# A new order of every engine's queue in a fused attention and feed-forward kernel, with other scratch tiles for one weight conversion

## The chip, the cores and the metric

One core of one Trainium2 chip runs the kernel. The metric is the device time of one execution in microseconds (us). Smaller is better. The kernel before took 1261.1 us (median of three runs, 1261.0 to 1261.12).

## The reference

Four batches of 12608 queries, keys and values of width 128 meet 49 agents. The attention result goes, row by row, through a feed-forward block with a SoLU activation.

```python
a2k = sm(agents, k)          # softmax(scale * agents @ k.T), per batch
agent_v = a2k @ v
q2a = sm(q, agents)
x = q2a @ agent_v            # 50432 rows of 128
h = x @ w_in                 # 1024 wide
sm = softmax(h)
solu = h * sm
ln = (solu - mean(solu)) / sqrt(var(solu) + 1e-06) * g_ln
out = ln @ w_out             # 50432 rows of 128, float32
```

`w_in` and `w_out` are float64 and come to the chip as pairs of 32-bit words. The kernel turns them into float32 with integer operations of its own.

## The kernel before, in words

The rows are cut into 394 tiles of 128. A tile's main path goes through five engines: PE multiplies it into two halves of a 1024-wide PSUM tile `ph` (`c_h`, L956), DVE takes the row maximum and writes a scaled copy to `e` (`c_max`, L984), ACT takes the exponential back into `ph` (`c_exp`, L991), DVE multiplies the two into one of six tiles `u_a` to `u_f` (`c_u`, L999), and ACT sums squares (`c_sq`, L1020). For eleven of thirteen tiles POOL then splits `u` into two float16 halves `f` (`c_f0`, L1007, and `c_f1`, L1010), SP has them transposed by DMA into `x` (`c_x`, L1014), and PE multiplies by the output weights (`c_w`, L1048). The other two of thirteen are transposed on PE (L1027) and copied into `t` (L1032). DVE scales four tiles at a time into an output buffer (`c_fin`, L1093), of which there are two, each for eight tiles, and SP stores it (`c_out`, L1099).

Before the first tile can run, the head of the kernel computes `agent_v` of batch 0 (`phase_a`, L567). It goes through twelve chunks of 1024 keys and one shorter one. For chunk c: SP loads k (`kload`, L585) and v (`vload`, L591; three small loads at L596 for the last chunk); PE multiplies k by the agents (`p1_mm`, L602); DVE takes a running maximum (L607, L614); ACT the exponential (`p1_exp`, L628); PE transposes it (`p2_t`, L635); ACT copies that out (`p2_et`, L645); PE multiplies it by v (`p2_mm`, L655); DVE adds it to `av` (`p2_ev`, L664). In the head k lies in the eight `x` tiles and v in the eight `t` tiles, so v of chunk 8 may be loaded once `p2_mm` of chunk 0 is done, v of chunk 9 after `p2_mm` of chunk 1, and so on up to chunk 12. Results of PE lie in four PSUM banks `px`; each product or transpose takes one and holds it until it is read. When all thirteen chunks are added up, `f1` (PE, L711), `f2` (ACT, L714), `f3` (PE, L745), `f4h` (ACT, L751) and `f4l` (DVE, L755) form the matrix that `c_h` uses.

The head also holds the conversion of both weights (L399, DVE, ACT and POOL), the centring of the output weights (POOL, L453, L462 and L472, with the PE product `mean`, L466, and DVE's `peak`, L477), and the softmax of the first eight tiles of queries (`phase_b`, L850: PE L864, DVE L870 and L876, ACT L880, POOL L894 and L898, PE L905, copy into `pT` L911).

The conversion `pair_f64` (L378) needs four scratch tiles, called s, a, e and m. For `w_in` they are `e_a`, `e_b`, `u_a`, `u_b`. For `w_out` they are `e_a`, `e_b`, `u_e`, `u_f`: it shares two with `w_in`, so all of its steps wait for the conversion of `w_in` (`cin` in L1132). The first two `c_max` write `e_a` and `e_b`, and the first six `c_u` write `u_a` to `u_f`, so L1174 and L1177 name both conversions, `cin + cout`, as what they wait for.

The order in which each engine gets its work is written out: `STEPS` (L25) is a packed list with one entry for each of 7003 steps, and `Plan.run` (L198) issues them in that order. Some steps may go to one of two engines, and a bit of the entry says which. Where the plan expects PE to idle in the head, `idle` (L1106) puts small products of constants into PE's queue, called fills here (L1109); their number follows from the plan. The kernel before has 57 of them.

Of the kernel before, what the change touches and what calls it, by code (L numbers as in the profile page):

```python
# [30 lines left out]
    "b0(`=m&fKE6V~f@8p08Nx2DgncV(swk+r(>(OCShXEV2suMe9o<k{`T@bI2?>|WN2RaFNg0Qh5D{U+RRO~&s|bv^&#JL~fA{noB-w?}-sNX#p%"
    "bk~>Krnq8qczs+FZf(zWWn$)tg6JV)k!t_o;v}fin1f>7t!}?-cxG`Yg^xCYRM%v`JG0bxHzZFP$A(Uf^8mjypESfKW#oA-MmiSOhBnSUiPiV("
    "!Be1<x7DiW{ijQ5^SR7);9vTUKj>~eX^_h2-)#(?D~UmT3-te^pSX;8vc1~95iL%hYbqxl(e{x;EQ9YK#k!QkUDK@tGO#)8kS7y^`;{HUpzm&a"
    "-|osNEOwvNxVo89kqIy{{cFFD-;>RkO^rw6HeE+OxM|S2kL2T^uevQ`8DBiPNH))XB&HS`O{)#S*)EgM`hm=5kRMJ0%PMv(op-cadsNGw8UL+&"
    ";Y3BW17KdOGP#I8ebnXd#SFTMrHsp-A;#}BEhI6Si{5QIZwObP-ku&Exgj(=rt7xf`TF|s=oxXUBxGxK26^Uz7(dZ~shhqep_;VqSh3*J1o-*?"
    "G4!G8oYdLf@>QQcdT3f1=olh;gS`X2aj@-mrcQ@?S{LtBZ6_1P(aW^uT73&D<m;WAJ`?d|B$VgMG0(9jBd<QuUlSbw;PRc0?S3#7HuYwd^X~?T"
    "ul;xg293CTW9F*yu&ZiM|NPsv?V-$s6pY|=58;d%^zBX8&D_-bYzy6*ba-^u>1?uCy=iFkaJ54UJRg^5FIJXjo!6@_Fq<Rlr{|{U%*MEwOnc|_"
    "GFLd9w%Y>n`0yQ}+A~f&<%ZCN*SJz2(N_3xS1p!?$GY}-*yx|WlASk%awFFY>{{_aHU!469|`^Bh|v}}scBv(T4IK@nq0kI-+g#gN&=4E@Y0#-"
    "nmG8N9KKepH=O;IA738_#{_5w<57!jL<XvzRbvgup^hD*s?iwMs2af714gbcpJI#2h*jDMLXPuG7+p0V35{k+9viXyfFpHuf`fVWQc8Vyo;mA{"
    ")wWbzM@MJ8(lyd}ELW_!vLRKg{H|s|KbrGTx1Gk~PQva#Z39xG);kK8vYscOqhiIjwh_-n$@<*~nKQH4Yye^7{KV2+@B;cKaM^BpknQQ0N1XRF"  # L40
    "%k!sR|GdMlvkxlGih;-Qk-X8|u+mm_5K<-N_}Z1m8<Ly0Mmu^f;<^UMXy8P1E&t&kbQ~)c?&g#nuatTFALceDBAE{#+BVzj@2A?r);5K;b~aOU"
    "i=SgnRU>-QPu^B9O;z51kWKi!mdX>&Q~;zl^c`1{di<<)uRfbmCHyUOw&_*(kqWHd1Po5O0tWQqS?}3do9);C)AXGtv~m+#bN}csHD?n2AI^8C"
    "30tz3Xj<J^x{8hB0N2z_LfDu$Tz;InO4PLj+fis|%|*PouPu*n>Z{c@*UjPZvK5R^YSY*9%GGzy*#*$ycPidbE>1eyNB;eP9>2mtqVHPa$OIkE"
    "-LuJT`%Odi(FBeXPH@}-dhHM=rJaH8h`KIvxzRm7qio*EWCw`8mI>SBK*x5)R?wQ6mUaZDC%TWfT8HKDClry{b>f}Wn7Hjc5KqZNiWq2;=+vaP"
    "bN1|{Zr&1Bdhn5n(F40C*P!lSoLp2#&8Au9T=<CS#(nnt+&M9T&$ODnnJysDsl3X$#iUYs(Q!m%Gu>TBonCwZZ#~<>@A{XOU;W683QsxWgzUU#"
    "a94LgBt7qIYl*>Sza<-4#Ld+!k&UUA-6g+uHgMChIB8k!-&X}Rj(ISAD{+M^z#|_CIC^7Czw^Bl`DpX|a3~!)?zn0X*ns0Ye3sQ8yZ-*)HM?aS"
    "2c|k@)kFP>D++qYjQV8=C182{FlzQh4*QQ!>N~uoZb94j-LEC=F7@b<;%F9Fb8Qd^W_yR5j(hf{!)Kd%>Df2{1HeAlo1L|WdiFO59a?gKt1DjV"
# [188 lines left out]
def kernel(  # L236
# [864 lines left out]
    def F(f, *x):  # L1101
        return lambda *y: f(*x, *y)
# [195 lines left out]
```

## Time and profile before

| what | us |
|---|---|
| median of three runs | 1261.1 |
| the profiled execution's own time | 1258.08 |
| span of that execution, first to last instruction | 1256.3 |
| first `c_max` starts, in the span | 57.83 |

The profiled execution was 3.0 us shorter than the median. Its span is counted from its first instruction. An engine's row of a view gives a start, a duration, the engine, the line, the operation, the tile written and the tiles read. In views by window, each engine's busy time in the window stands with the number of its instructions. SPq is the queue of DMA issues.

### The profile page before, as it was taken

Reading aid. Unit: us, or ns where it says so; the run is one execution under the profiler, and the core shown is the slowest. Engines: PE = TensorE matmul, PEld = TensorE weight load, DVE = VectorE, ACT = ScalarE, POOL = GpSimd, SP = SyncE. Lnnn points to the kernel's source line nnn. Section 1 sums busy time; section 2 is a strip of 40 time slices with the busy share of each in tenths; the row PEclk is TensorE's granted clock in tenths of the full one; section 3 lists DMA queues with packets and bytes.
Section 4 is the critical chain, followed back from the end, with each engine's and each line's share of the span. In section 5 each row is a group of like instructions: output and inputs, shape, how many; then the busy total and the mean of one; then the engine's idle time right before and its main releaser. Section 6 shows DMA issues by size and latency. Waiting matters only on the chain.

```text
span 1256.3 us, 36417 instructions
## 1 busy us (share of the span) xinstructions
PE 1211.7 (96%) x14324; PEld 935.4 (74%) x14324; DVE 1202.1 (96%) x2296; ACT 1181.9 (94%) x2210; POOL 1120.3 (89%) x891
## 2 busy tenths in 40 slices
PE   8889999999999999999999999999999999999998
PEld 4667777777777877777778777777777777777778
DVE  5799999999999999999999999999999999999997
ACT  5499899999999999999999999899999999999998
POOL 3488898999999998889999989889898999999995
PEclk9999999999999999999999999999999999999999
DMA  9589999999999999999999999999999799899897
GB/s 366 202 195 242 229 246 232 239 249 201 202 210 239 243 231 250 246 257 221 229 205 207 247 243 227 240 259 217 230 231 195 173 200 198 189 218 199 176 209 169
DMA packets 721516, 281.41 MB, mean 224 GB/s; under 512 B 692672, under 2 KB 696256, under 8 KB 721344
## 3 DMA queue, kind: packets, MB, share of 16 engines
q1 hardware_dynamic: 721344, 279.08, 103.5%
q8 instruction: 112, 1.84, 0.6%
q14 instruction: 60, 0.49, 0.1%
HBM read 79.67 MB, written 25.82 MB: 84 GB/s over the span
## 4 chain that ended last, share of the span: by engine, by line
PE 27%; DVE 21%; ACT 19%; issue 14%; POOL 10%; DMA 9%; SPq 0%; POOLq 0%; DVEq 0%; ACTq 0%
PE px L1048 11%; ACT ph L991 8%; PE ph L956 7%; DVE e_b L984 4%; DVE e_a L984 4%; ACT sq_b L1020 4%; ACT sq_a L1020 3%; PE px L655 2%; PE px L602 2%; DVE u_c L999 2%; POOL f_a L1010 2%; DVE u_d L999 1%; DVE u_b L999 1%; DVE u_a L999 1%; DVE u_e L999 1%
## 5 line engine op out<-in xcount | busy, mean ns | idle before, releaser
L984 DVE TENSOR_SCALAR_CACHE_REDUCE e_a<-ph,nk 128x1024 f32<-128x1024 f32 x197 | 251.8, 1278 | 7.4 <-PE ph L956 6.4
L984 DVE TENSOR_SCALAR_CACHE_REDUCE e_b<-ph,nk 128x1024 f32<-128x1024 f32 x197 | 251.7, 1278 | 3.9 <-PE ph L956 3.3
L991 ACT ACTIVATE ph<-e_a,nm 128x1024 f32<-128x1024 f32 x197 | 219.2, 1113 | 15.2 <-DVE e_a L984 13.8
L991 ACT ACTIVATE ph<-e_b,nm 128x1024 f32<-128x1024 f32 x197 | 219.3, 1113 | 8.2 <-DVE e_b L984 7.3
L999 DVE SCALAR_TENSOR_TENSOR u_d<-e_b,cb,ph 128x1024 f32<-128x1024 f32 x66 | 84.2, 1276 | 2.1 <-ACT ph L991 1.7
L999 DVE SCALAR_TENSOR_TENSOR u_a<-e_a,cb,ph 128x1024 f32<-128x1024 f32 x66 | 84.1, 1274 | 1.8 <-ACT ph L991 1.4
L999 DVE SCALAR_TENSOR_TENSOR u_c<-e_a,cb,ph 128x1024 f32<-128x1024 f32 x65 | 82.8, 1274 | 2.2 <-ACT ph L991 1.9
L999 DVE SCALAR_TENSOR_TENSOR u_e<-e_a,cb,ph 128x1024 f32<-128x1024 f32 x65 | 82.9, 1275 | 1.3 <-ACT ph L991 1.1
L999 DVE SCALAR_TENSOR_TENSOR u_b<-e_b,cb,ph 128x1024 f32<-128x1024 f32 x65 | 83.0, 1276 | 1.0 <-issue 0.3
L999 DVE SCALAR_TENSOR_TENSOR u_f<-e_b,cb,ph 128x1024 f32<-128x1024 f32 x65 | 82.8, 1274 | 0.9 <-ACT ph L991 0.4
L1048 PE MATMUL px<-wh,x_c 128*128 128x128 f16 x672 | 70.9, 219 | 2.9 <-DMA x_c<-f_e 2.2
L1048 PE MATMUL px<-wh,x_a 128*128 128x128 f16 x672 | 70.3, 219 | 3.0 <-DMA x_a<-f_c 1.2
L1048 PEld LDWEIGHTS <-x_c 128*128 128x128 f16 x1008 | 61.9, 98 | 13.5 <-DMA x_c<-f_e 3.0
L1048 PEld LDWEIGHTS <-x_a 128*128 128x128 f16 x1008 | 61.5, 98 | 14.0 <-DMA x_a<-f_c 1.8
L1048 PE MATMUL px<-wh,x_b 128*128 128x128 f16 x672 | 71.3, 219 | 0.0
L1048 PEld LDWEIGHTS <-x_b 128*128 128x128 f16 x1008 | 61.4, 98 | 12.9 <-issue 4.9
L1048 PE MATMUL px<-wh,x_h 128*128 128x128 f16 x656 | 69.3, 219 | 1.7 <-DMA x_h<-f_a 1.7
L1048 PEld LDWEIGHTS <-x_d 128*128 128x128 f16 x984 | 60.5, 98 | 13.8 <-issue 2.7
L1048 PEld LDWEIGHTS <-x_e 128*128 128x128 f16 x984 | 60.2, 98 | 14.1 <-issue 3.8
L1048 PEld LDWEIGHTS <-x_h 128*128 128x128 f16 x984 | 60.5, 98 | 13.6 <-DMA x_h<-f_a 2.2
L1048 PE MATMUL px<-wh,x_d 128*128 128x128 f16 x656 | 68.9, 219 | 1.1 <-ACT ek_b L628 0.4
L1048 PE MATMUL px<-wh,x_e 128*128 128x128 f16 x656 | 68.9, 219 | 0.8 <-DMA x_e<-f_a 0.6
(455 smaller groups left out, 4731.9 us busy)
## 6 DMA issues: line engine op xcount, KB each, us to landing
qt_a<-in_qT_dram SPq DMA_DIRECT2D x24, 512.0 KB, 5.0
qt_b<-in_qT_dram SPq DMA_DIRECT2D x24, 512.0 KB, 5.1
out_dram<-ob_a SPq DMA_DIRECT2D x24, 512.0 KB, 4.0
out_dram<-ob_b SPq DMA_DIRECT2D x24, 512.0 KB, 3.6
kt_b<-in_kT_dram SPq DMA_DIRECT2D x18, 512.0 KB, 4.8
kt_a<-in_kT_dram SPq DMA_DIRECT2D x18, 512.0 KB, 5.4
vt_b<-in_v_dram SPq DMA_DIRECT2D x18, 512.0 KB, 5.2
vt_a<-in_v_dram SPq DMA_DIRECT2D x18, 512.0 KB, 4.6
```

The costliest lines, as they stand in the source:

```text
L602: nc.tensor.matmul(px[h * AP2 : (h + 1) * AP2, :w], ag_sb[:, b, :], kt[:, o : o + w], start=True, stop=True)
L655: nc.tensor.matmul(px[h * AP2 : (h + 1) * AP2, :C], eT[:w, o + h * AP2 : o + (h + 1) * AP2], vt[:w, t, :], start=all(z[0] != h for z in mm ...
L956: nc.tensor.matmul(ph[:, sl], w, m[:, sl], start=(q == 0), stop=(q == len(mm) - 1))
L984: nc.vector.tensor_scalar(out=nhs[x], in0=phs[x], scalar1=nks[k][:, j : j + 1], scalar2=None, op0=ALU.mult, op1=ALU.min, accum_out=nms[x])
L991: nc.scalar.activation(out=phs[x], in_=nhs[x], func=AF.Exp, scale=-1.0, bias=nms[x], accum_out=rs_[R]["S"][:, j : j + 1])
L999: nc.vector.scalar_tensor_tensor(out=u, in0=nhs[x], scalar=scal(x)[:, 4:5], in1=phs[x], op0=ALU.mult, op1=ALU.mult, accum_out=su)
L1010: nc.gpsimd.tensor_tensor(out=fs[x][:, 1, :], in0=us[x][0], in1=fs[x][:, 0, :], op=ALU.subtract)
L1020: nc.scalar.activation(out=sq, in_=u, func=AF.Square, bias=su, scale=-float(DF), accum_out=rs_[R]["Q"][:, j : j + 1])
L1048: nc.tensor.matmul(po, ut, wt[:, kf, :], start=(q == 0), stop=(q == len(mm) - 1))
```

## The change

The scratch of `w_out`'s conversion becomes `u_c`, `u_d`, `u_e`, `u_f`. It no longer shares a tile with that of `w_in`, so its steps drop `cin` as a dependency, `c_max` of the first two tiles waits for `cin` alone, and so does `c_u` of tiles 0 and 1; `c_u` of tiles 2 to 5 waits for `cout`. The packed list is another one over the same 7003 steps.

```diff
 STEPS = (
...
 )
...
-            for k, tg in zip("saem", er + (ur[:2] if names == "in" else ur[4:])):
+            for k, tg in zip("saem", er + ur[:2] if names == "in" else ur[2:]):
...
-    cout = [chain(c_out_f[h], OUTC, [res["wout"]] + cin) for h in range(2)]
+    cout = [chain(c_out_f[h], OUTC, [res["wout"]]) for h in range(2)]
...
-        MX[x] = op("D", F(c_max, x, ku - 1, t % UB), 1.2, ..., [H[x, 0], H[x, 1], NK] + (cin + cout if x < 2 else []))
+        MX[x] = op("D", F(c_max, x, ku - 1, t % UB), 1.2, ..., [H[x, 0], H[x, 1], NK] + (cin if x < 2 else []))
...
-        U[x] = op("D", F(c_u, x), 1.205, ..., [EX[x], CB[b]] + used + (cin + cout if x < UBUF else []), after=[U.get(x - 1)])
+        U[x] = op("D", F(c_u, x), 1.205, ..., [EX[x], CB[b]] + used + (cin if x < 2 else cout if x < UBUF else []), after=[U.get(x - 1)])
```

Unpacked, the two lists put the loads of the head on SP in this order (k and v with the chunk; q0 the first queries, wi and wo the weights):

```
before: wi k0 k1 k2 q0 k3 k4 k6 v6 k5 wo k7 v0 k8 v1 k9 v2 k10 v3 v4 v5 k11 k12 v7 v8 v9 v10 v11 v12 q1 q2
after:  wi k0 k1 q0 k2 k4 k3 k6 v6 k5 wo v0 k7 v1 v2 k8 v3 k9 k10 v4 k11 v5 k12 v7 v8 v9 v12 v11 v10 q1 q2
```

PE's order in the head (P = p1_mm, T = p2_t, M = p2_mm with the chunk; b0 = L864; pk = the two transposes of L905; a number in brackets is a count of fills):

```
before: [14] P0 P1 [6] b0 T0 P2 [3] T1 P3 [14] T2 P4 T3 P5 [3] T4 P6 T5 P7 M0 pk [4] T6 pk P8 M1 T7 [1] P9 M2 T8 [3] P10 M3 M4 T9 [2] T10
        M5 P11 P12 M6 M7 g1 M8 g3 T11 T12 M9 mean f0 M10 M11 M12 [4] f1 [3] q2
after:  [14] P0 P1 b0 [2] T0 P2 T1 [2] P3 [3] T2 P4 [1] T3 P5 [5] T4 P6 [2] M0 [1] T5 P7 M1 T6 M2 P8 T7 M3 P9 T8 P10 M4 T9 P11 T10 P12
        M5 M6 M7 M8 g1 M9 g3 T12 T11 mean M10 f0 M11 M12 pk pk f1 [3] q2
```

The list after has 33 fills. It puts `pk` and its two copies, both on ACT now, straight ahead of `f1` and `f2`; the second part of the second group's softmax (DVE, L876) behind the first two `c_max`. Behind the head the two lists differ by swaps of near neighbours. Of the steps that may go to either of two engines, DVE gets 16 copies into `pT` (before 20) and 9 into `t` (before 6).

The stores of eight tiles, counted by how many tiles past its last one the latest transpose ahead of a store is: six stores before are 18 or more tiles late (those of tiles 40, 200, 216, 232, 296 and 312), nine after (8, 104, 136, 152, 232, 264, 296, 312 and 328). The store of tiles 200 to 207 goes from 21 to 8.

## Rows read from the trace of the kernel before

**Rows 1.** The page: busy time, share of the span and instructions of each engine.
```profile
span 1256.3 us, 36417 instructions
PE 1211.7 (96%) x14324; PEld 935.4 (74%) x14324; DVE 1202.1 (96%) x2296; ACT 1181.9 (94%) x2210; POOL 1120.3 (89%) x891
```

**Rows 2.** Windows: busy time by engine in each, granted clock, DMA share, GB/s.
```profile
0.00:57.80 57.80, 50.94 (x453) 30.78 (x453) 37.09 (x109) 27.77 (x68) 23.03 (x34) 1.00 0.77 292
57.80:1230.00 1172.20, 1137.77 (x13600) 883.45 (x13599) 1146.98 (x2157) 1133.88 (x2104) 1085.75 (x840) 1.00 1.06 222
1230.00:1256.30 26.30, 23.02 (x275) 21.13 (x272) 18.00 (x33) 20.22 (x39) 11.57 (x18) 1.00 0.70 163
```

**Rows 3.** Windows within the head, the same columns: PE, PEld, DVE, ACT, POOL.
```profile
8.60:27.55 18.95, 18.93 (x131) 9.09 (x132) 13.50 (x36) 11.34 (x28) 6.34 (x6) 1.00 1.04 411
27.55:51.38 23.83, 22.85 (x258) 16.65 (x258) 16.20 (x47) 11.97 (x36) 13.27 (x14) 1.00 0.74 289
36.00:38.00 2.00, 2.00 (x32) 1.49 (x30) 2.00 (x5) 0.66 (x2) 1.06 (x1) 1.00 1.02 418
40.00:42.00 2.00, 2.00 (x26) 1.43 (x27) 0.36 (x2) 1.25 (x3) 1.94 (x3) 1.00 1.07 329
46.00:48.00 2.00, 2.00 (x27) 1.65 (x25) 0.50 (x4) 1.41 (x5) 0.00 (x0) 1.00 0.03 8
```

**Rows 4.** The chain that ended last, in order of time, in the head.
```profile
25.67 1.01 PE px L602 x4
26.68 0.87 PE px L655 x16
...
27.88 0.44 PE ph L1109 x4
...
48.02 2.83 PE px L655 x38
...
51.39 0.46 PE px L711 x2
51.88 0.28 ACT av_dup L714
...
57.26 0.57 DVE logits L876
57.83 1.20 DVE e_a L984 x2
```

**Rows 5.** SP's queue: what its issues waited for, from 27.55 to 45 us.
```profile
SPq L591 <- PE px L655: 5.2, 2, 3.3
```

**Rows 6.** Timeline of the head (chunk 2's exponent, copies, centring), and one copy near the end.
```profile
18.58 0.70 ACT L628 ACTIVATE ek_a<-px,nmp 128x512 f32<-128x512 f32 x1
...
19.77 0.60 PE L635 MATMUL px<-ident,ek_a 128*128 128x128 f32 x4
...
29.24 0.43 DVE L911 COPY pT_b<-px 128x512 f16<-128x512 f16 x1 [0.96 <-PE px L905]
...
39.17 0.57 ACT L911 COPY pT_a<-px 128x512 f16<-128x512 f16 x1
...
50.58 1.25 POOL L472 TENSOR_TENSOR f_e<-f_e,mean_sb 128x512 f32<-128x512 f32 x1
...
1243.33 0.68 DVE L1032 COPY t_e<-px 128x512 f32<-128x512 f32 x1
```

**Rows 7.** Windows behind the head, all engines: the most and the least idle hundred of DVE.
```profile
700.00:800.00 100.00, 95.97 (x1153) 73.75 (x1152) 94.22 (x177) 93.13 (x173) 88.70 (x67) 1.00 1.16 237
1000.00:1100.00 100.00, 95.71 (x1173) 75.66 (x1172) 99.23 (x179) 99.15 (x179) 97.58 (x74) 1.00 0.94 199
```

**Rows 8.** Timeline of SP and DVE around two late stores.
```profile
774.39 0.53 SPq L1099 DMA_DIRECT2D out_dram<-ob_a  x1
774.98 0.42 SPq L1099 DMA_DIRECT2D out_dram<-ob_b  x1
...
779.51 0.69 DVE L1093 TENSOR_TENSOR ob_b<-px,yc 128x512 f32<-128x512 f32 x1 [1.23 <-DMA out_dram<-ob_b]
...
789.95 1.28 DVE L984 TENSOR_SCALAR_CACHE_REDUCE e_a<-ph,nk 128x1024 f32<-128x1024 f32 x1 [1.94 <-PE ph L956]
```

**Rows 9.** Waits of DVE from 58 us to the end: total us, times, longest.
```profile
DVE ob_b L1093 <- DMA out_dram<-ob_b: 1.2, 1, 1.2
```

**Rows 10.** Windows around the first tiles: PE idles, then runs at a lower granted clock.
```profile
57.80:61.70 3.90, 1.64 (x37) 1.42 (x36) 3.90 (x11) 3.26 (x5) 1.45 (x2) 0.98 0.53 165
61.70:65.00 3.30, 3.30 (x14) 1.68 (x14) 2.71 (x5) 3.30 (x8) 3.17 (x2) 0.50 0.21 86
```

More of the change, by code (lines that the diff above doesn't have):

```diff
@@ L31 @@
[L31 to L35, printed above, removed]
@@ L146 @@
[L146 to L150 removed]
+    "c-ozL4@@gtdf)ii_;Pu-x5$||^H@SDL6le)a#@zJ1R=^=j>|fPScFnUsN*`su@FKCAwpQ!YdM4<L=o!{*K#e#B9tPRP~<qS*Fh8^L|Kax<Perp"
@@ new lines @@
+    "L<#kd9E%Xb<#LUg={YlFd&a)6-Sk}^%*>fN=R4oO-|zcQ<8d>dR4S95<rjvY15g#~INxp|+BOMg?a@Yia4RIck6xL}BmMVtja}~p=GyW89raG{"
+    ")xgkTxy;q?RCO%R1k~}Kqp{!$eB#)SCR+yWsoICY<lW_7z*$#*)pT@UcX?ux#qOImM=NzVy%+Bi>hkEr(ad{a@8LslR8v0H<k)|YPgVB;&*atL"
+    "e*M1Q>Wh_c?TowLk5;Ug_uNp;hW9mPmkH@aNast;$U-T@oxFT#_#ySKH#NR`ho4=xjjrv#SH)+++L>~<6C_fOdW)N~+igI<CC&6yIVBRUD&dm="
+    "jgm^q&otyk+YV5Z$xIU&*Cds`q4-IYnoJ!U&z0nV`C1||O-3X)wO8t@dUr2ADgIIunn;}t4*F9QK-tu}pgc<sM&q;5!7<b6?&hKakMF3*r<OZM"
+    "bw@w^QKvE)Cl>sb3wT_uy?L%(RZJQDTIFK!<l-j2Mv#L;2K7+i{c2rv#SeaK^>BS+(VKZc0Olij2Gf?w5|w}Wa(_If@-)Y$=GBwa=TDJkAd}C&"
@@ new lines @@
+    "E4z;@NbTxm+&~bg<xAs@LrckyxWdxhDkJ)b6B?o)0Aqt<cG#~`T!dB0&E4ciVy>fgckArN5Z_r(9uV=v?KZheo1C9Nqf%iY3sA@L(Aq!%>ziBv"
+    "_;Ab^B>Vx7ZmWt=s!mUuPZEuar1k_0r!>UuH-6+<35IvyKav)3Ox^gp>dPM-(Y=n%`s;&aVp6}~zV|fSu5AzWX(!f)db<qKfiq=C<r--}o0;A9"
+    "Z#ys7T)i{5hE7wNJ}RH_;rEn+`k()>eK|SQIyY@q5xoFdToYEG=43>-<eLThg^+RRdHwzL45@eN6n>%#%#dDueEH&TW$U;(H9i_0oB{VsmBaH>"
+    "HuAIw2f$EQ-q>mg*=+}o@a5<)ek+yST3o*It@J*~>aOAq{WEd`gvrKf5Aj?F8obA<mg^=Es`qxcT<Gq*oXOh9fAmf3RX2HNXdUeCUrNOycvF4L"
+    "=%&o)pS~Sh*C}R=9n*t<_T7W2vDK}Wk^QCqKDjP|o0Iim{Mcyl%z(PR3VV;dqSnx41I~%`0Z#dzoENQToq}53GOLIh0Gu{rtJRI4+Nb7?+grn%"
@@ L151 @@
+    "kQQXx;)Z0dJyw7?bWsmONHGMozCe{l{NyvOuFud!A(0SvoC+y%5p^nLa9A;eEozow0*;J*hCpC+At?~b%%_n>^_rkU6jp?M_DTz~bYT(rxq=ug"
+    "AZc`A7mxmmBJZn@*7#z7jvEMj2}N?zg&nnmHg93ev#9;c<JH1uGfmS13=rgVVWGe$WuG}(`%E7hD{2Y}5Q`S@5c)F-yU68ey13==ncfD56($Zr"
+    "2`=op7qnzBA&<j~8XG_M(Hi}gM{9+y^!cMTUa5qAw!upm76$^@F4#F%SUd?kP(`h)LVqcW%fb$75#9Mr&$ghm_hTHb@jT`$j@ATrD=-ePlSCIa"
+    "QNQYFO?W2s)eY0aqqU;Oqp+J(#1{YFM{D%o=V-0a<pdc1|97<Ze*l6(As_"
 )
@@ L1173 @@
             NK = op("D", F(c_nk, ku - 1, x, m), 0.15 * (1 + both(x)), dues[3] + 0.4, [rsum["op", ku - 1], CB[b]])
-        MX[x] = op("D", F(c_max, x, ku - 1, t % UB), 1.2, at(x, DMX + (0.0 if xbar(x) else DMXF), DMXR, DMXL), [H[x, 0], H[x, 1], NK] + (cin + cout if x < 2 else []))
+        MX[x] = op("D", F(c_max, x, ku - 1, t % UB), 1.2, at(x, DMX + (0.0 if xbar(x) else DMXF), DMXR, DMXL), [H[x, 0], H[x, 1], NK] + (cin if x < 2 else []))
         EX[x] = op("A", F(c_exp, x), 1.132, at(x, DEX + (0.0 if xbar(x) else DEXF), DEXR, DEXL), [MX[x], U.get(x - 2), FIN.get(RS0[rgrp[x][0] - 3] // GT - 1 if rgrp[x][0] > 3 else -1)], after=[EX.get(x - 1)])
         used = [T.get((x - UBUF, 0)), T.get((x - UBUF, 1)), SQ.get(x - UBUF), F1.get(x - UBUF)]
-        U[x] = op("D", F(c_u, x), 1.205, at(x, DU_ + (0.0 if xbar(x) else DUF), DUR, DUL), [EX[x], CB[b]] + used + (cin + cout if x < UBUF else []), after=[U.get(x - 1)])
+        U[x] = op("D", F(c_u, x), 1.205, at(x, DU_ + (0.0 if xbar(x) else DUF), DUR, DUL), [EX[x], CB[b]] + used + (cin if x < 2 else cout if x < UBUF else []), after=[U.get(x - 1)])
         SQ[x] = op("A", F(c_sq, x), 1.14, at(x, DSQ + (0.0 if xbar(x) else DSQF), DSQR, DSQL), [U[x]] + ([om] if not x else []))
```

230 lines of the change are left out of this document (110 added, 120 removed).

## The prediction

> **What bounds the kernel now.** I read the page first. Over the whole span PE, DVE, ACT and POOL are busy 96, 96, 94 and 89 per cent [rows 1], so no single engine is to be relieved, and the question is where the idle time lies. The windows answer that [rows 2]. Of DVE's 54.2 us of idle time, 20.7 lie in the head (57.80 less 37.09) and 8.3 in the last 26.3 us. The 1172.2 us between hold 25.2, or 2 per cent. The head is therefore where an order can bring most: up to the first `c_max` none of the 394 tiles has advanced, and each microsecond by which it starts sooner moves the rest by as much, if the rest keeps its pace.
>
> What bounds the head is seen in its windows [rows 3]. In the middle (36 to 38 us) the loads run without a gap, at 418 GB/s, and PE is full too. From 40 us the loads ebb, and at 46 us there are none (8 GB/s); yet PE is full until `f1` at 51.38. So PE ends the head, not the loads, by some 5 us. The chain of waits says the same: products of v (L655) follow on each other up to `f1` [rows 4]. PE was late with them because v comes late in SP's list: v of chunk 0 behind k of chunk 7. The same lateness comes back to SP: two loads of v waited 5.2 us together until an earlier product had freed their tile [rows 5].
>
> **The change, part by part.** I make the sum in the profiled execution's own time, 1258.08 us; the median of the runs is 3.0 us longer, and the same difference is taken off it.
>
> *Loads.* The bytes are the same. Each v moves up by one place, and in the new list v of chunk 12 (three issues), 11 and 10 come in this order. Chunk 12's needs `M4` done, and 11, 10 and the two q loads stand behind it on SP. By then (about 36 us) loads issued earlier still keep DMA full [rows 3], so that the wait need not show. I cost it at nothing, covered by PE's work on chunks 5 to 9; without that cover it is at most the 5.2 us of [rows 5].
>
> *PE up to the product of v's chunk 0.* PE is busy 18.93 of 18.95 us here [rows 3], fills among it: 26 before, 16 after (without the 14 ahead of P0). A fill takes 0.44/4 = 0.11 us [rows 4], so ten fewer are 1.1 us. But they stand where PE waits for an exponent: from an exponent's start on ACT to the transposes that need it go 1.19 us (18.58 to 19.77), and exponents come one by one [rows 6]. With fills gone, mostly the wait remains. Following the new order by these durations, P0 to P7, T0 to T5 and M0 are done at 27.3 instead of 27.55. I take 0.25, with 0 and 1.1 as ends.
>
> *PE from there to `f1`.* Before, this is 23.83 us: 22.85 busy, 0.98 idle [rows 3], and 14 fills, 1.5 us. That leaves 21.3 us of work, which both orders hold (each of P, T and M as often, `pk` too). After, there are no fills. Idle remains where T6 to T9 wait for their exponents: between P of a chunk and its T stand one or two other pieces, a P or M of 1.01 us each [rows 4], against maximum, exponent and 1.19. I allow three waits of 0.25, 0.75 in all: 22.1 us, a gain of 1.75. The ends: nothing if all fills turn into waits, 2.5 if none does and the 0.98 goes too.
>
> *`pk` and its copies.* They move from the middle to just ahead of `f1` and `f2`. PE's part is counted above. On ACT two copies of 0.57 [rows 6] now stand in front of `f2`, which before started 0.5 us behind `f1` [rows 4]. The first starts when the first transposes are out, so about 0.3 us stick out and delay `f2`. Ends: 0 and 1.1, both copies. Waiting behind `f2` are `f3`, `q1` and all of the first tiles.
>
> *DVE ahead of the first `c_max`.* 0.57 us (L876) [rows 4] go behind it, and small steps of 0.4 or so come ahead. As DVE is full from there on, this only changes places: +0.1 for the start, nothing for the end. Centring on POOL, which ends 0.45 us after `f1` starts before (50.58 + 1.25) [rows 4, 6], moves up with the conversion and stays covered by `f1` to `q1`.
>
> *The scratch tiles.* Removed: `w_out`'s wait for `w_in`. It costs and gives nothing by itself; it lets DVE do these steps sooner, under loads. Added: `c_u` of tiles 2 to 5 wait for a conversion done some 20 us earlier, so nothing.
>
> *Steps that changed engines.* DVE loses four copies of 0.43 and gains three of 0.68 [rows 6]: +0.3 us over 1200. ACT and POOL change as little. Nothing.
>
> *All behind the head.* The same work in an order of swapped neighbours. I can't price this from a row, so I bound it: DVE's most idle hundred holds 5.8 us of idle time, its least 0.8 [rows 7]. If one hundred went from one end half way to the other, that is 2.5 us either way. I take 0, as neither direction has a reason.
>
> Sum: 0.25 + 1.75 - 0.3 + 0.1 = **1.8 us** sooner. The profiled execution would take 1256.3 us, the median 1261.1 - 1.8 = **1259.3 us**. Ends from the head alone: 1.1 + 2.5 + 0.1 = 3.7 sooner, and no gain. A measurement of this kernel can tell about 0.2 per cent, 2.5 us, from no change, so my forecast counts as the same.
>
> **The rivals.**
>
> *The head packs tightly.* All fills and waits go, and 3.7 us come off: 1257.4. For it: PE has 24 fewer fills, 2.6 us by themselves. Against it: fills stand in waits, and T still waits for ACT. Chance 0.17.
>
> *A stall far behind goes too.* Two stores of eight tiles were issued side by side at 774 us; DVE waited 1.23 us for an output buffer, and 1.94 us for PE some 10 us later [rows 8]. In the new list the first of them comes 13 tiles sooner. 1.8 + 1.23 + 1.94 = 5.0, so 1256.1. Against it: other stores come late instead. Chance 0.15.
>
> *A new wait eats the head's gain.* `f2` waits the full 1.1 for both copies, and the fills all turn into waits for exponents: 1261.1. Chance 0.14.
>
> *Late stores: slower.* Nine stores come 18 or more tiles late, six before. `c_fin` of a buffer's next use stands in DVE's queue in order, and all main steps of DVE behind it wait with it. Before, one late pair showed the stall, 1.23 + 1.94 = 3.2 us [rows 8]. If two such stalls come on top, 6.3 are lost and 1.8 won: 1265.6. From one on top the result is slower than my forecast, from two it is slower than before by over 0.2 per cent. Against it: DVE waited for a store only once [rows 9], so five of the six late ones cost it nothing. Chance 0.07.
>
> *PE's clock falls in the head.* Behind the first products of tiles PE was idle for 2.26 of 3.9 us, and the next 3.3 us went at a granted clock of 0.50, that is at 1.2 GHz instead of 2.4 [rows 10]. If the missing fills let that happen once in the head, 3.3 us at half speed cost 1.65, and 1260.9 is left. Against it: by my working no wait in the new head is longer than 0.9 us, and before, 0.98 us of idle time in 23.83 left the clock at 1.00 [rows 3]. The Trainium skill (TensorE: Matmul & The Clock Gate, "What's actually happening") speaks against the change here: it calls the throttled clock the default, which activity releases, and fewer fills are less activity; by that rule alone the result would be this rival's. The trace bears the rule out behind the head [rows 10], not in it [rows 3]. Chance 0.05.
>
> *The change doesn't do what it says*: not possible here for the order, as the list is what is issued; for the scratch it would show in nothing.
>
> **How the numbers follow.** The forecast has the remaining 0.42: 0.08 of it faster by over 0.2 per cent (head nearer to its upper end), 0.32 the same, 0.02 slower. Faster: 0.08 + 0.17 + 0.15 = 0.40. Same: 0.32 + 0.14 (gain eaten) + 0.05 (clock) = 0.51. Slower: 0.02 + 0.07 = 0.09. The range takes the forecast with 2.5 us either way, and reaches down to the stall that goes (1256.1) and 1.3 below, as both gains of the head may come together with it: 1254.8. Up it goes to the eaten gain with part of the bound on the rest, 1262.8. Left out are late stores and the far ends, less than 2 in 10.
>
> **What would show it right or wrong.** `f1` should start near 49.4 us instead of 51.39, with P12 done before M5; no wait of SP for a product of v longer than before; the two copies right ahead of `f2`; first `c_max` near 55.9. If DVE's idle time from there to 1230 us stays near 25, the forecast holds. A granted clock below 1.00 ahead of `f1`, `f1` later than 50.5, or waits of `c_fin` for `out_dram` in several places would make it wrong; so would a first `c_max` at 56 with a total that is 3 or more us off.

## The result: the head gained what was forecast, the rest lost several times as much

| | before | after |
|---|---|---|
| median, us (7 runs each) | 1261.1 (1256.85 to 1265.82) | 1268.85 (1265.08 to 1273.63) |
| ratio, 95% interval | | 1.0065 [1.0048, 1.0082] |
| the profiled execution's own time | 1258.08 | 1265.08 |
| its span | 1256.3 | 1263.3 |
| first `c_max` starts | 57.83 | 56.10 |

The time is 7.75 us over that of before, and so outside the forecast's range. The kernel is slower, by 0.65 per cent, and the interval leaves no doubt about the direction. The seven runs of before lie up to 9.0 us apart, so that one pair of times would not have told this.

The page of after, which answers to [rows 1]:

```profile
span 1263.3 us, 36367 instructions
PE 1214.8 (96%) x14300; PEld 937.5 (74%) x14300; DVE 1202.3 (95%) x2295; ACT 1180.4 (93%) x2209; POOL 1121.5 (89%) x893
```

DVE is busy as long as before (1202.3 and 1202.1 us): no work was added. The windows of after, cut at its own first `c_max`, say where it idles. Columns as in [rows 2].

```profile
0.00:56.05 56.05, 48.28 (x428) 29.13 (x429) 37.73 (x109) 28.10 (x70) 23.60 (x34) 1.00 0.79 300
56.05:1230.00 1173.95, 1136.57 (x13523) 882.01 (x13521) 1139.10 (x2142) 1126.79 (x2093) 1079.46 (x836) 1.00 1.04 221
1230.00:1263.30 33.30, 29.96 (x352) 26.33 (x350) 25.49 (x45) 25.48 (x47) 18.49 (x24) 0.99 0.80 172
```

Subtract DVE's busy time from each window. In the head it idles 18.3 us (before 20.7), in the last window 7.8 (8.3). In the middle it idles 34.9 (25.2): all of the loss, 9.7 us, lies there, where the forecast had put nothing. What DVE waited for in the middle (in total, times, longest):

```profile
DVE e_a L984 <- PE ph L956: 10.1, 19, 1.4
DVE pk L718 <- ACT av_dup L714: 4.4, 3, 1.5
DVE av L664 <- PE px L655: 3.7, 2, 3.1
...
DVE ob_a L1093 <- DMA out_dram<-ob_a: 0.7, 1, 0.7
```

The first three lines in the kernel before:

```profile
DVE e_a L984 <- PE ph L956: 6.4, 13, 1.9
DVE pk L718 <- ACT av_dup L714: 1.6, 3, 0.9
DVE av L664 <- PE px L655: 1.2, 1, 1.2
```

The waits for PE and ACT grew, in many places. The wait for a store did not: 0.7 us once, where before it was 1.2 once [rows 9].

The 3.1 us are the longest single wait. SP's queue ahead of it:

```profile
265.78 2.88 SPq L1014 DMA_TRANSPOSE x_d<-f_b  x1
268.77 1.59 SPq L596 DMA_DIRECT2D vt_b<-in_v_dram  x3
270.41 0.58 SPq L843 DMA_DIRECT2D qt_a<-in_qT_dram  x1
271.09 0.38 SPq L1099 DMA_DIRECT2D out_dram<-ob_b  x1
271.56 0.38 SPq L1099 DMA_DIRECT2D out_dram<-ob_a  x1
271.99 1.17 SPq L591 DMA_DIRECT2D vt_a<-in_v_dram  x1
273.25 5.53 SPq L1014 DMA_TRANSPOSE x_e<-f_c  x1
```

The chain that ended last and the timeline show what came of it:

```profile
273.25 9.06 DMA x_e<-f_c
```

```profile
282.35 0.23 PE L1048 MATMUL px<-wh,x_e 128*128 128x128 f16 x1 [3.25 <-DMA x_e<-f_c]
285.15 0.35 DVE L664 SCALAR_TENSOR_TENSOR av<-av,fc_l,px 128x128 f32<-128x128 f32 x1 [3.10 <-PE px L655]
```

Seven plain issues, loads and stores, stand between two transposes. The second transpose lands 9.06 us after its issue began; PE, in order, waits 3.25 us for it, and DVE 3.10 behind PE. In the old list the same plain issues stand in two groups, of five and two, with transposes between.

The granted clock had a part in the 3.10 us:

```profile
283.10:286.50 3.40, 3.40 (x27) 2.50 (x26) 1.13 (x5) 1.36 (x4) 3.32 (x3) 0.50 1.25 278
283.12 1.97 PE L655 MATMUL px<-vt_a,eT_a 128*64 128x128 f32 x16
```

Right behind its wait PE ran at 0.50, that is at 1.2 GHz instead of 2.4. The sixteen products that DVE waited for took 1.97 us; sixteen of the same shape take 1.09 in the head, at 1.00 (35.65 below). So about 0.9 of the 3.10 us came from the clock.

**The head.** The timeline around `f1` in after:

```profile
32.74 1.45 POOL L399 TENSOR_TENSOR u_f<-u_f,u_d 128x512 f32<-128x512 f32 x1
33.24 1.50 DVE L399 SCALAR_TENSOR_TENSOR u_c<-f_d,u_c 128x512 int32<-128x512 int32 x1
...
35.65 1.09 PE L655 MATMUL px<-t_e,kt_b 128*64 128x128 f32 x16 [1.20 <-DVE av L664]
...
49.40 0.58 ACT L911 COPY pT_a<-px 128x512 f16<-128x512 f16 x1 [2.93 <-PE px L905]
49.56 0.46 PE L711 MATMUL px<-ff,av 128*128 128x128 f32 x2
49.88 0.59 ACT L911 COPY pT_b<-px 128x512 f16<-128x512 f16 x1
50.35 0.28 ACT L714 COPY av_dup<-px 128x128 f32<-128x128 f32 x1
...
56.10 1.28 DVE L984 TENSOR_SCALAR_CACHE_REDUCE e_a<-ph,nk 128x1024 f32<-128x1024 f32 x1
```

`f1` starts at 49.56 (before 51.39), and the first `c_max` 1.73 us sooner (1.65 by its start in DVE's timeline, 57.74 before, which the table below uses). That is the forecast's 1.8. SP's waits for products of v went from 5.2 us [rows 5] to 3.9, though the longest is 3.5 where it was 3.3:

```profile
SPq L596 <- PE px L655: 3.9, 2, 3.5
```

From there on the starts of `c_max` (L984) can be set beside those of before, tile by tile; a positive number is time lost. The row is one profiled execution of each kernel.

```
tile        0     36     48     60     84     96    180    204    252    288    393
after    -1.6   -2.4    0.9    0.9    8.2    7.8    9.3    9.2    6.8    7.4    8.8
```

The lead is lost between tiles 36 and 48, and between 60 and 84 some 7 us more.

### The profile page after: what moved, and what is told of

The parts are those of the page before. It is cut to its first block, busy times and chain, and to the rows that moved or that the text cites. A ratio compares the mean times of both kernels' runs of the same rounds, so it can differ in the third digit from the quotient of the medians.

```text
span 1263.3 us, 36367 instructions
## 1 busy us (share of the span) xinstructions
PE 1214.8 (96%) x14300; PEld 937.5 (74%) x14300; DVE 1202.3 (95%) x2295; ACT 1180.4 (93%) x2209; POOL 1121.5 (89%) x893
## 4 chain that ended last, share of the span: by engine, by line
PE 28%; ACT 22%; DVE 16%; POOL 13%; issue 11%; DMA 9%; SPq 0%; POOLq 0%; ACTq 0%; DVEq 0%
PE px L1048 12%; ACT ph L991 9%; PE ph L956 7%; ACT sq_b L1020 4%; ACT sq_a L1020 4%; DVE e_b L984 3%; DVE e_a L984 3%; PE px L655 2%; POOL f_d L1010 2%; PE px L602 2%; POOL f_e L1010 2%; POOL f_c L1010 2%; PE px L1027 2%; DMA x_e<-f_c 2%; DVE u_a L999 1%
## 5 line engine op out<-in xcount | busy, mean ns | idle before, releaser
L984 DVE TENSOR_SCALAR_CACHE_REDUCE e_a<-ph,nk 128x1024 f32<-128x1024 f32 x197 | 251.8, 1278 | 11.1 <-PE ph L956 10.5
L984 DVE TENSOR_SCALAR_CACHE_REDUCE e_b<-ph,nk 128x1024 f32<-128x1024 f32 x197 | 251.8, 1278 | 3.9 <-PE ph L956 3.2
L1048 PE MATMUL px<-wh,x_g 128*128 128x128 f16 x656 | 68.1, 219 | 2.1 <-DMA x_g<-f_a 1.1
```

The source lines that it names most:

```text
L984: nc.vector.tensor_scalar(out=nhs[x], in0=phs[x], scalar1=nks[k][:, j : j + 1], scalar2=None, op0=ALU.mult, op1=ALU.min, accum_out=nms[x])
L1048: nc.tensor.matmul(po, ut, wt[:, kf, :], start=(q == 0), stop=(q == len(mm) - 1))
```

## The experiments

Most kernels carry both lists and put together their own: steps of the first list up to some place, then those of the next that are not yet issued, and so on (`new` is the changed kernel's list, `old` that of before; 249 steps are the head). All have the new scratch tiles unless the text says otherwise. The edits are shown shortened.

```diff
-        todo = steps()
+        new, old = steps(), steps(OLD)
+        todo = []
+        for part in (...):
+            done = dict(todo)
+            todo += [z for z in part if z[0] not in done]
```

Each was timed beside the kernel before on the same chip, whose medians were 1259.3 to 1260.1 us. One profile can be several us off another of the same order, so verdicts rest on the ratios; profiles show places. A ratio is a kernel's time over that of the kernel before, so 0.001 is 1.26 us.

**Head and rest apart.**

```diff
+        for part in (new[:249], old):
```

> Edit: the first 249 entries of the new list (all up to the first c_max), then all that is left in the order of the old list. Theory 'behind the head' (the head's gain of 1.6 us is real, and all of the loss comes from the new order behind it): the first c_max near 56.1 us, DVE's idle time from there as before, a median 1.7 us below that of the kernel before, ratio 0.9987. Rival 'the head upsets what follows' (an earlier start shifts loads against transposes): first c_max at 56.1 us too, but the loss is there: 5 to 8 us above before, ratio 1.004 to 1.0065.

Measured: 1257.73 us, ratio 0.9975 [0.9959, 0.9991], the first `c_max` 1.06 us sooner and the last 1.29.

```diff
+        for part in (old[:249], new):
```

> Edit: the first 249 entries of the old list, then all that is left in the order of the new one. Theory 'behind the head': first c_max near 57.8 us, and 8.7 us more of DVE idle time behind it, most between 170 and 330 us: 8 to 10 us above before, ratio 1.0065 to 1.008. Rival 'the head upsets what follows': with the old head the new order behind it loses nothing: within 2 us of before.

Measured: 1270.95 us, ratio 1.0087 [1.0066, 1.0108]. The two effects add up: 1.0087 and 0.9975 together give 1.0062, and the change measured 1.0065. The new head brings 2 to 3 us, and the new order behind it costs (1.0087 - 1) x 1260 = 11. Each of the two carries the new scratch tiles as well, so the sum counts them twice; that it still agrees with the change leaves nothing for them, within some 4 us.

**SP's order alone.** Behind the head's 34 issues, SP's queue follows one list and all other engines the other.

```diff
+        sp = [SP's steps of new][:34] + [SP's steps of old][34:]
```

> Edit: the new list on every engine, but SP's queue behind its first 34 issues in the old list's order. Theory 'bunched issues' (loads and stores stand side by side on SP ahead of transposes, these come late, and PE and DVE wait): the stall of 3.1 us near 282 us is gone, DVE's idle time from 170 to 330 us falls by 6 or more, and the median lies between 2 us below before and 2 above. Rival 'other queues' (the order on PE, DVE, ACT and POOL loses the time by itself): 5 to 9 us above before as with the whole change, ratio 1.004 to 1.007.

Measured: 1281.8 us, ratio 1.0165 [1.0142, 1.0187].

```diff
+        sp = [SP's steps of old][:34] + [SP's steps of new][34:]
```

> Edit: the old list on every engine, but SP's queue behind its first 34 issues in the new list's order. Theory 'bunched issues': the late transposes come with SP's order, so 5 to 9 us above before, ratio 1.004 to 1.007, the first c_max at 57.8. Rival 'other queues': within 2 us of before.

Measured: 1276.97 us, ratio 1.0124 [1.0098, 1.0151]. Both are slower than either list whole, and slower than theory or rival foretold. An order of SP fits only the other queues that it was planned with, so this pair can't tell whose order was at fault. It does show that SP's order alone is worth 13 to 16 us, with all compute in place: (1.0165 - 1.0065) x 1260 and (1.0124 - 1) x 1260.

**The group of seven issues.** SP's places 122 to 131, around the group shown above, from the other list.

```diff
+        sp[122:132] = [SP's steps of old][122:132]
```

> Edit: the whole new list, but the ten SP issues of places 122 to 131 in the old list's order. In the new order six loads and stores (eight DMAs) stand between the transposes of tiles 61 and 62; in the old one the same ten are split by transposes. Theory 'bunched issues': PE's wait of 3.3 us for the transpose of tile 62, near 282 us, and DVE's of 3.1 behind it go; the kernel is 3 to 4 us faster than the whole change (5 to 8 us above before becomes 1.5 to 4.5 above, ratio 1.001 to 1.0035). Rival 'no single place' (many small late transposes, each absorbed or not from run to run): within 1.5 us of the whole change, ratio 1.004 to 1.0075.

(The expectation counts eight transfers; the rows above show seven.)

Measured (in the changed kernel): 1265.96 us, ratio 1.0052 [1.0033, 1.0072], against 1.0065. This is in the rival's range.

```diff
+        sp[122:132] = [SP's steps of new][122:132]
```

> Edit: the new head and the old order behind it, with the same ten SP issues in the new list's order. Theory 'bunched issues': DVE waits some 3 us near 280 us behind the transpose of tile 62, and 3 to 4 us are lost against the run with the new head alone: ratio 1.000 to 1.0015. Rival 'no single place': no more than 1 us from the run with the new head alone, ratio 0.997 to 0.9985.

Measured (in the kernel with the new head alone): 1259.19 us, ratio 0.9997 [0.9977, 1.0016], against 0.9975. Made in an order without it, the group costs (0.9997 - 0.9975) x 1260 = 2.8 us; the two intervals overlap, but the profile shows the place: it falls back 4.1 us between tiles 60 and 84, where that of the new head alone falls 0.1. Split in the changed kernel, it brings 1.6 by the same sum, less than the intervals can tell. It is one place of several.

**Stretches.**

```diff
+        for part in (new[:871], old[:1818], new):
```

> Edit: the new list up to the first step of tile 36's c_max, then the old order up to tile 90's, then the new one again. Theory 'batch 1's loads' (the time is lost between 170 and 330 us, where batch 1's k and v share SP and the DMA engines with the transposes): the loss goes, from 3 us below before to 1 above, ratio 0.9975 to 1.001. Rival 'no single place': the loss falls by about the share of this stretch, a seventh, and 4 to 7 us above before stay, ratio 1.003 to 1.006.

Measured: 1266.59 us, ratio 1.0059 [1.0041, 1.0077]. The old order from tile 36 to 90 gave nearly nothing back, as the rival said; the profile falls back by 4.3 us between tiles 36 and 48, on the old order.

```diff
+        for part in (new[:249], old[:876], new[:1819], old):
```

> Edit: the new head, the old order up to tile 36's c_max, the new one up to tile 90's, the old one to the end. Theory 'batch 1's loads': most of the loss comes back: 5 to 8 us above the run with the new head alone, ratio 1.0025 to 1.005. Rival 'no single place': 0 to 2 us above that run, ratio 0.9975 to 0.999.

Measured: 1262.75 us, ratio 1.0027 [1.0009, 1.0045]: 6.6 us over the new head alone, as the theory said, lost between tiles 60 and 96 in the profile (-3.0 to 5.1).

```diff
+        for part in (new[:871], old):
```

> The new order up to c_max of tile 36, the old one from there to the end. Theory (the loss between tiles 36 and 48, which shows in each kernel that has the new order of tiles 1 to 36, whatever order follows, and in none that has the old one there, comes from that new order, which leaves the transposes on SP late): c_max of tile 48 falls back by 3 to 4 us against that of tile 36, and the time is 3 to 4 us over the kernel with the new head alone, a ratio of 1.000 to 1.001. Rival (the loss belongs to the order behind tile 36): no fall there, a ratio of 0.997 to 0.998.

Measured: 1263.09 us, ratio 1.0029 [1.0005, 1.0053], 6.8 us over the new head alone. Between tiles 36 and 48 the profile falls from -2.63 to 1.27. So the theory holds for the place: the loss there is made ahead of tile 36 and shows behind it, as in the kernel with the old order from 36 to 90. The time is 6.8 over and not 3 to 4; the intervals leave some 3 us either way. The waits of PE and DVE from 168 to 215 us name the cause:

```profile
PE px L1048 <- DMA x_d<-f_c: 3.6, 1, 3.6
DVE e_a L984 <- PE ph L956: 4.8, 1, 4.8
```

With the new head alone these two are 0.7 and 0.6. SP issued that transpose at 174.78 us instead of 171.72, and behind PE's wait the granted clock was 0.51 from 184.0 to 187.4 us. A wait can stand far from its cause.

```diff
+        for part in (new[:249], old[:1916], new[:3388], old):
```

> The head in the new order, the old order up to c_max of tile 96, the new one up to c_max of tile 180, the old one to the end. Theory (the new order loses time at several separate places, one of them between tiles 96 and 180): the starts of c_max, against those of the kernel before, fall back by 4 to 5 us between tiles 96 and 180, as in the changed kernel, and the time is 4 to 5 us over the kernel with the new head alone, a ratio of 1.000 to 1.002. Rival (what is lost there follows from time lost earlier, between tiles 36 and 96, which is in the old order here): no fall, a ratio of 0.996 to 0.998.

Measured: 1257.9 us, ratio 0.9991 [0.9968, 1.0014]. The fall between tiles 96 and 180 is 3.0 us (-2.02 to 0.97), but the kernel with the new head alone falls by 0.9 there too. That leaves some 2 us, which the intervals do not show.

```diff
+        for part in (new[:249], old[:6605], new):
```

> The head in the new order, the old order up to c_max of tile 372, the new one from there to the end. Theory (in the tail the new order puts a c_fin ahead of work that DVE could do, where it waits for POOL): the last c_max starts as in the kernel with the new head alone, about 1.3 us sooner than before, or 0.5 later than that, and the end comes about 2 us later than with the new head alone: a ratio of 0.999 to 1.000. Rival (that wait in the tail is slack, for something else ends last): 0.997 to 0.998.

Measured: 1255.77 us, ratio 0.9968 [0.9951, 0.9985]. The rival holds: the wait in the tail is slack. This is the lowest ratio of the kernels with the whole computation, but no further from the new head alone than the intervals reach; both lie below the kernel before by their intervals, and so below both kernels of the case.

```diff
+        for part in (new[:249], old[:4131], old[4309:4310], old):
```

> The head in the new order, all behind it in the old one, but for one step on SP: the store of tiles 200 to 207 is issued 12 tiles sooner, alone between two transposes. Theory (the stall of 1.23 us of DVE for the output buffer at 774 us and the 1.94 us for PE behind it are that store's doing): both go and nothing takes their place, so 2.5 to 3.2 us come off the time with the new head alone: a ratio of 0.9945 to 0.996, and c_max of tile 252 starts about 4 us sooner than before. Rival (DVE would wait there for PE in any case, as the transposes behind are what is late): under 1 us, 0.997 to 0.998.

Measured: 1256.3 us, ratio 0.9973 [0.9956, 0.9989]. The rival holds. The stall at 779 us [rows 8] belongs to one execution: the kernel with the new head alone has the same order there, waited for a store 0.6 us in its whole profile, and its `c_max` of tile 252 starts 2.1 us sooner, against before, than that of tile 228.

```diff
+        for part in (new[:249], old[:3670], new[:4649], old):
```

> The head in the new order, the old order up to c_max of tile 196, the new one up to c_max of tile 252, the old one to the end. Theory (the new order behind the head isn't worse everywhere: between tiles 216 and 250 it gains 3.5 us): c_max of tile 252 starts 4 to 5 us sooner than before, a ratio of 0.994 to 0.996, the fastest of all. Rival (the gain seen there in the changed kernel was only time that its queues, late already, did not lose a second time): 0.997 or more.

Measured: 1257.0 us, ratio 0.9973 [0.9953, 0.9994]. The rival holds: no gain from that stretch.

By ratios against the new head alone, the stretches cost 6.8 (up to tile 36), 6.6 (36 to 90), 2.0 (96 to 180), -0.3 (196 to 252) and -0.9 us (from 372): 14.2 us where the whole rest costs 11. Each is uncertain by some 3 us, and tiles 180 to 196 and 252 to 372 were not tried by themselves. Nearly all of it comes from the first 90 tiles, in which SP also carries the loads of batch 1. A full queue alone does not make the loss, though. SP carries the loads of batches 2 and 3 later, and in the changed kernel it was issuing 95 to 96 per cent of the time from 420 to 480 us and from 720 to 840, in stretches where the new order costs 2.0 us and nothing.

**Stores off SP.** The 52 stores go through ACT's queue.

```diff
-        nc.sync.dma_start(out=out[:, x0 * C : x1 * C], ...
+        nc.scalar.dma_start(out=out[:, x0 * C : x1 * C], ...
```

> The changed kernel, but its 52 stores are issued from ACT's queue, at the same place of the list, and not from SP's. Theory (what the new order loses behind the head, it loses because transposes are late behind plain issues on SP): with a third of the plain issues gone from SP, some 60 to 90 us of SP's issuing time go, the waits of PE for transposed tiles shrink, and DVE's wait for PE (10.5 us behind the head in the changed kernel) falls to 6 or less; against that ACT gets 52 issues of about 0.5 us in its queue, 26 us, of which a part shows. If half of ACT's part is hidden, the time is near 1268.9 - 5 + 3. In any case the distance to the next kernel (old order behind the head, the same edit) shrinks from 11 us to under 5. Rival (the loss lies in the order of PE, DVE, ACT and POOL themselves): the distance stays near 11.

Measured: 1272.8 us, ratio 1.0102 [1.0069, 1.0135].

> The kernel with the new head alone, its 52 stores issued from ACT's queue. Theory: as in the changed kernel with this edit, transposes are issued sooner, but here they were late seldom, so that ACT's issues cost more than they bring: 2 to 8 us slower than with the stores on SP, and under 5 us ahead of the changed kernel with the same edit. Rival: as much slower as the changed kernel is with this edit, or as much faster, so that 11 us stay between the two.

Measured: 1261.32 us, ratio 1.0015 [0.9985, 1.0044]. The distance between the orders stays at 0.0087 x 1260 = 11 us, as the rival said, with some 6 us of uncertainty either way. But the theory's premise fell with it. SP's issues behind 58 us took 967 us in the changed kernel with this edit and 968 without it, though the 52 stores alone had taken 27; with the new head alone they fell by 12, from 952 to 940. There were fewer issues, and each transpose was longer (behind another transpose 2.22 us in place of 2.08, in both orders). The longer ones are those beside a store: with the edit, a transpose behind another took 3.0 and 2.9 us (38 and 40 times) where a store from ACT's queue was under way at its start, and 2.1 elsewhere. So a transfer holds up a transpose whichever engine issued it. The Trainium skill (DMA: Bandwidth & Descriptors, "Issuing engines are not separate DMA queues") says that transfers started by several engines run on the same 16 DMA engines and only issuing time is saved; this pair agrees, and of the issuing time less than half was saved in one order and next to none in the other. So the pair could not tell the theories apart.

**Small loads.** What could: take the large transfers away, in all orders alike. The loads of k and v from chunk 2 of batch 1 on, and of q from the fifth group on, bring 16 columns; the output from there is that of other inputs. Issues and compute stay (in these kernels line numbers are 4 or 5 higher).

```diff
+            if b > 1 or b == 1 and c > 1:
+                w = 16
             nc.sync.dma_start(out=kts[c][:, :w], in_=kT[b, :, c * CT * P : c * CT * P + w])
...
+            if c < NCK and (b > 1 or b == 1 and c > 1):
+                nc.sync.dma_start(out=vt[:, 0, :16], in_=v[b, : P, :16])
+            elif c < NCK:
...
-            nc.sync.dma_start(out=qts[k][:, : c1 - c0], in_=qT[:, c0:c1])
+            n = c1 - c0 if k < 4 else 16
+            nc.sync.dma_start(out=qts[k][:, :n], in_=qT[:, c0 : c0 + n])
```

> The kernel before, but the loads of k, v and q behind the first ones bring 16 columns in place of 1024 (k and v from chunk 2 of batch 1 on, except v's last chunk; q from the fifth group on), so the output is that of other keys, values and queries from there; the number of issues and all work of the compute engines stay. Theory (transposes on SP take long because large transfers are under way, and SP's queue, 95 per cent full from 120 to 240 us, holds up PE and then DVE): a transpose behind plain issues takes 2 to 2.6 us and not 3 to 6, SP's queue is 15 to 25 per cent emptier, PE's waits for transposed tiles nearly go, and the time falls by 3 to 10 us. Rival (SP's queue is slack): the time falls by less than 2.5.

Measured: 1243.61 us (1242.48 to 1245.37), ratio 0.9861 [0.9834, 0.9888].

> The new head with the old order behind it, with the same small loads. Both theories: 1 to 3 us sooner than the kernel before with small loads, as the head's loads are as they were and its gain is kept.

Measured: 1242.25 us, ratio 0.9852 [0.9825, 0.9879].

> The changed kernel with the same small loads. Theory (the new order behind the head loses its 11 us through late transposes on SP): it comes within 4 us of the new head with the old order and the same small loads. Rival (it loses them in the order of PE, DVE, ACT and POOL, such as DVE's wait of 4.4 us for f2 at the three changes of batch): it stays 8 to 11 us behind.

Measured: 1246.59 us (1245.18 to 1247.53), ratio 0.9886 [0.9864, 0.9908]. The kernel before gains 16 us, the theory's 3 to 10 being too little; the new head keeps 1.4 of its gain; and the changed order is now 4.3 us behind it instead of 11. So about 7 of the 11 us come through the large loads, with some 3 us of uncertainty, and 4.3 are left without them: theory and rival each have a part.

SP's queue shows the first part. The kernel before, a group of four loads ahead of a transpose:

```profile
170.31 0.53 SPq L591 DMA_DIRECT2D vt_a<-in_v_dram  x1
170.89 0.42 SPq L585 DMA_DIRECT2D kt_a<-in_kT_dram  x1
171.36 0.42 SPq L591 DMA_DIRECT2D vt_b<-in_v_dram  x1
171.83 0.43 SPq L585 DMA_DIRECT2D kt_b<-in_kT_dram  x1
172.36 7.07 SPq L1014 DMA_TRANSPOSE x_d<-f_c  x1
```

The same issues with small loads:

```profile
167.92 0.53 SPq L593 DMA_DIRECT2D vt_a<-in_v_dram  x1
168.50 0.42 SPq L587 DMA_DIRECT2D kt_a<-in_kT_dram  x1
168.98 0.42 SPq L593 DMA_DIRECT2D vt_b<-in_v_dram  x1
169.44 0.43 SPq L587 DMA_DIRECT2D kt_b<-in_kT_dram  x1
169.97 1.32 SPq L1019 DMA_TRANSPOSE x_d<-f_c  x1
```

The plain issues take the same; the transpose behind them takes 1.32 us in place of 7.07. What it waits for is seen in the time that the last of the four loads takes from issue to landing, in the kernel before:

```profile
kt_b<-in_kT_dram SPq DMA_DIRECT2D x1, 512.0 KB, 7.8
```

Issued at 171.83, it landed at 179.6; the issue of the transpose ended at 179.43. In that trace, behind 60 us, 102 of the 107 transposes that follow plain issues ended their issue within 0.5 us of the landing of the last of these. SP can issue nothing in the meantime. Added up over SP's rows, its queue was issuing 96 per cent of the time from 120 to 180 us and 94 from 180 to 240 in the kernel before (95 and 94 after); with small loads 68 and 65. PE's waits for transposed tiles fell from 9.5 us behind the head to 0.4 (in the changed order from 11.3 to nothing). With full loads the two orders differ by 1.9 us in the sum of these waits; what reached DVE were the long ones, such as the 3.25 us above.

The second part is seen in DVE's waits with small loads: the new head with the old order first, then the changed order.

```profile
DVE pk L722 <- ACT av_dup L718: 1.6, 3, 0.9
```

```profile
DVE pk L722 <- ACT av_dup L718: 4.4, 3, 1.5
DVE e_a L989 <- PE ph L961: 2.6, 7, 0.5
DVE e_b L989 <- PE ph L961: 2.1, 3, 1.1
```

The 1.6 and the 4.4 are the same as before and after with full loads. One of the three places, in the changed order:

```profile
297.96 1.28 DVE L989 TENSOR_SCALAR_CACHE_REDUCE e_a<-ph,nk 128x1024 f32<-128x1024 f32 x1 [0.55 <-PE ph L961]
299.29 1.12 ACT L996 ACTIVATE ph<-e_a,nm 128x1024 f32<-128x1024 f32 x1 [0.98 <-DVE e_a L989]
300.44 0.24 ACT L718 COPY av_dup<-px 128x128 f32<-128x128 f32 x1
300.71 0.29 DVE L722 TENSOR_REDUCE pk<-px 128x1 f32<-128x128 f32 x1 [1.46 <-ACT av_dup L718]
```

and in the old one:

```profile
301.18 0.25 ACT L718 COPY av_dup<-px 128x128 f32<-128x128 f32 x1
301.45 0.29 DVE L722 TENSOR_REDUCE pk<-px 128x1 f32<-128x128 f32 x1 [0.19 <-ACT av_dup L718]
```

The new list puts `q1` (L722) on DVE straight behind a `c_max`, and `f2` (L718) on ACT behind the exponent of that very tile. DVE has to sit out the whole exponent, 1.46 us at each of the three changes of batch. In the old list a `c_u` stands between at the place shown, and covers it. These neighbours cost 4.4 - 1.6 = 2.8 us of DVE's time. The rest of the 4.3 was not traced to single places.

## Why the prediction was wrong, point by point

**The head was right in sum, and the split wrong.** Forecast: 0.25 us sooner up to the product of v's chunk 0, 1.75 more up to `f1`, 0.3 back at `f2`, 0.1 at DVE. Measured: P0 to P7, T0 to T5 and M0 were done at about 26.46 in place of 27.55 (P7, the last of them, started at 25.48), so the first term was about 1.1, its upper end (fills removed, not turned into waits). From there to `f1` PE took 23.10 us in place of 23.83, a gain of 0.73 and not 1.75. PE idled 1.5 us, and mostly not for exponents: one wait of 1.20 us was for `av` on DVE, longer than the 0.9 us that the prediction's working allowed. `av` stood behind a step of the output weights' conversion (L399) that took 1.50 us beside one of POOL's. Before, the same step took 0.69, with POOL idle:

```profile
36.11 0.69 DVE L399 SCALAR_TENSOR_TENSOR e_a<-f_d,e_a 128x512 int32<-128x512 int32 x1
```

So the conversion, which the prediction put at no cost, had a part in that wait. That the two terms add up to nearly the forecast's 2.0 is luck. The loads were misread too: "each v moves up by one place" holds for v0 and v1 alone; v2 and v3 move up by two, v4 and v6 to v9 stay and v5 falls back by one. `f2` started 0.79 us behind `f1`, 0.3 more than before, as forecast, and 6.54 us lay between `f1` and the first `c_max` where 6.44 did. The granted clock stayed at 1.00 in the head, so the rival of a falling clock did not occur there. Experiments gave the head 1.4 to 3.1 us.

**The step that failed** is "All behind the head": "I take 0, as neither direction has a reason", bounded by "2.5 us either way". It measured 11 us slower. Two things were wrong in it. The bound was drawn from one hundred of DVE's idle time, as if one place could change; swaps of neighbours stand in every part of the list, and tiles up to 90 alone cost more than the bound. And there was a reason for a direction. Behind the head the new list has 47 transposes that follow two or more plain issues, the old one 39. SP's queue had little slack where batch 1 is loaded, 96 per cent from 120 to 180 us; this stands in the timeline of SP alone, since the page doesn't count issuing as busy. The step on loads looked at SP in the head only, where loads in a row cost it little. Behind the head the same loads stand between transposes, and a row of before shows what that can cost SP (7.07 us, among the longest there; PE waited only 0.4 us for that tile, so it reaches PE where no slack is left). No one priced a swap of a load with a transpose there. That these reasons make the direction is argued; that the loss lies in the order behind the head, and 7 of its 11 us go with the large loads, is shown.

**Late stores** was the one rival on the slower side, and its mechanism was not what happened: `c_fin` waited for a store 0.7 us once. Stores did cost, but by being in flight ahead of a transpose, along with the loads: in the kernel before a transpose took 2.64 us behind one store (28 times) and 2.09 behind another transpose. **A stall far behind goes too** named a stall that comes and goes between executions of the same order; moving its store changed nothing. **A new wait eats the head's gain** looked for it in the head, where there was none of that size.

The sign that was named as the refutation came: first `c_max` near 56, with a total more than 3 us off, and DVE's idle time from there to 1230 us at 34.9 and not 25.

Still open: which of the swaps ahead of tile 36 cost most, and how the 7 us divide among them. Nor was the clock's share taken apart. All eight profiles with the new order ahead of tile 36 have a second stretch at a granted clock of 0.50 that begins between 66 and 70 us, and none of the twelve with the old order there has one; in after:

```profile
68.00:71.40 3.40, 3.40 (x39) 2.79 (x38) 3.40 (x5) 3.40 (x7) 3.40 (x4) 0.51 0.62 247
```

The lead falls from 1.6 us at tile 4 to nothing at tile 8 there, and is back at tile 36. The stretches' sum (14.2 against 11) and the old order from 36 to 90, which gave nothing back, show that the costs are not independent of what comes before them.

## What to carry to other kernels

Look at the issuing queue as an engine: add up its rows in the timeline by stretch before calling a reorder of it free, since the page shows only compute. In this kernel a DMA transpose issued right behind large loads or stores held SP until these had landed, so count such neighbours in both orders, and look at which matmul needs the tile next. A full queue did not lose time everywhere, so the place still has to be found by experiment. Where two engines hand a small result to each other, one independent step in the consumer's queue can hide what the producer does first: it left DVE 0.19 us of 1.46 to wait here.

## What the runs showed of the hardware

Over the kernel before, behind 60 us, a transpose took 2.09 us on average to issue behind another transpose (223 times), 3.22 behind one plain issue (68), 4.29 behind two (20) and 5.45 behind three (10). With small loads these are 1.89, 1.95, 1.98 and 2.38. Behind four it took 4.30 (6 times) and behind five 3.55 (3 times): what counts is not the number of issues but when the transfers ahead have landed.

The spread from run to run goes with that traffic: in one session the kernel before ran from 1251.85 to 1264.83 us with full loads (11 runs), and with small ones from 1242.48 to 1245.37 (5 runs). The large loads cost this kernel 16 us of 1260, though the busy shares of the page hardly show them.
